# Five equal token blocks become four blocks of 512 local rows and one block of the 128 global rows

## The chip, the cores and the metric

One core of one Trainium2 chip runs the whole program. The metric is the device time of one execution in microseconds; the kernel before was run three times (890.51, 888.89 and 883.43 us, median 888.89).

## The reference

Attention with a band and global tokens feeds two feed-forward layers; 4 batches, 8 heads of 64, 512 local and 32 global positions each. Shortened:

```
k_all, v_all = [k_g, k_l], [v_g, v_l]                      # per batch and head
out_g = softmax(q_g @ k_all.T / 8) @ v_all                 # 32 global rows see all 544
s_ll  = where(|i - j| <= 32, q_l @ k_l.T / 8, -1e9)        # 512 local rows see a band
out_l = softmax([q_l @ k_g.T / 8, s_ll]) @ v_all           # ... and the 32 global keys
x = [out_g, out_l] as 4 * 544 = 2176 tokens of 512 features
h = x @ w_in            (512 -> 2048);  g = h if h > 0 else exp(h) - 1;          x = g @ w_out (2048 -> 512)
h = x @ w2_in           (512 -> 2048);  g = h if h >= 1 else 0 if h <= -1 else (h + 1)^2 / 4;  return g @ w2_out
```

Everything is float32. The kernel splits each factor of a layer's product into a high part and a low part (type float32r on the matmul) and forms a product by three matmuls: low weights with high activations, high with low, high with high.

## The kernel before, in words

**Attention (up to about 144 us).** 24 units of work (for each batch four pairs of heads of local rows and two quadruples of heads of global rows) run as a software pipeline whose order is written out by hand (class `Pinned`, line 109: instructions are kept in program order). A unit ends with transposes that lay its rows out as 128 features by tokens, and with `x_high` (line 281, ScalarE) and `x_low` (line 288, VectorE), which split them into the tiles `xh[j]` and `xl[j]` of token block `j`. The five blocks of 436, 436, 436, 436 and 432 tokens cut through the batches, so a unit's 512 local rows fall into two blocks and are copied in two pieces each (`spans`, line 63). Between the units, weights of the first three column groups are prepared and five products of the first layer are already computed (`early_ups`, line 608).

**Layers (from about 144 us).** Here instructions may be reordered by the scheduler of the language. A layer has 16 groups `f` of 128 of its 2048 inner features. They are taken in chunks of 3, 4, 3, 4, 2 (layer one) and 4, 3, 4, 3, 2 (layer two); within a chunk the loop runs over the token blocks `j` and inside over the `f` of the chunk (lines 700 to 718). One step (`f`, `j`) is:
- *up* (line 205): 12 matmuls, 4 slices of the contraction by 3 products, with 128 weight columns stationary and the tokens of the block moving, into one of four PSUM banks;
- `curve` and `join` (lines 211 to 228): the activation, two passes of ScalarE and one (layer one) or two (layer two) of VectorE;
- `high`, `low` (lines 230, 234): the split into `gh` (ScalarE) and `gl` (VectorE);
- *down* (line 270), three steps later (`LAG`): 12 matmuls, 4 output slices `d` by 3 products, into four banks `dn0` to `dn3`, which gather all `f` of the chunk;
- after the chunk's last `f`, `collect` (line 245): each bank is added to `acc[j]` on VectorE (the first chunk copies it on ScalarE). After the last chunk of layer one the sum is split again into `xh[j]`, `xl[j]` (lines 256, 257), after that of layer two it is written out, one transfer per block and slice (line 259).

**Weights.** Raw weights of one `f` are a transfer of 1 MB on the SP queue into a single raw buffer; two ScalarE and seven VectorE instructions then make the high and low tiles (`prep`, line 136). During a chunk, those of the next chunk are prepared, spread over its steps by `W_SHARE` (line 712). They go into a ring of seven tiles.

The code of the functions that the diff touches:

Of the kernel before, what the change touches and what calls it, by code (L numbers as in the profile page):

```python
# [58 lines left out]
W_SHARE = 0.8  # L59
WARM_UP = 10  # L60


def spans(t0, n):

    for j, (s, m) in enumerate(zip(STARTS, BLOCKS)):
        a, b = max(t0, s), min(t0 + n, s + m)
        if a < b:
            yield j, a - s, a - t0, b - a
# [3 lines left out]
def band_attention_then_two_mlps(  # L72
# [32 lines left out]
    xh = [xpool.tile([P, KT, n], F32R, name=f"xh{j}") for j, n in enumerate(BLOCKS)]  # L105
    xl = [xpool.tile([P, KT, n], F32R, name=f"xl{j}") for j, n in enumerate(BLOCKS)]
# [21 lines left out]
    slots = {}  # L128
# [3 lines left out]
    def add_slots(pool, numbers):  # L132
        for i in numbers:
            slots[i] = pool

    def prep(wraw_p, wtmp_p, layer, f, c0, n, raw_tag="wraw"):
# [5 lines left out]
        slot = (layer * NF + f) % WRING  # L142
        if (layer, f) not in wtiles:
            wtiles[layer, f] = [
                slots[slot].tile([P, WCOLS], F32R, tag=f"w{nm}{slot}", name="w" + nm) for nm in "hl"
            ]
# [41 lines left out]

    class Up:


        def __init__(self, layer, f, j):
            self.layer, self.f, self.j, self.n = layer, f, j, BLOCKS[j]
            self.k = 0
            early = count[0] < UP_EARLY or count[0] % 4 == 0
            count[0] += 1
            pool = ps_up[0 if early else 1]
            self.ps = pool.tile([P, BMAX], F32, tag="up", name="up")[:, :self.n]

        def products(self, m):  # L200
            wh, wl = wtiles[self.layer, self.f]
            for k in range(self.k, self.k + m):
                kt = k // 3
                w, x = ((wl, xh), (wh, xl), (wh, xh))[k % 3]
                eng.tensor.matmul(  # L205
                    self.ps, w[:, kt * P:(kt + 1) * P], x[self.j][:, kt, :],
                    start=k == 0, stop=k == 3 * KT - 1,
                )
            self.k += m

        def curve(self):
            self.g = t_p.tile([P, BMAX], F32, tag="g", name="g")[:, :self.n]
            if self.layer == 0:
                eng.scalar.activation(self.g, self.ps, AF.Exp)  # L214

                eng.scalar.activation(self.g, self.g, AF.Relu, bias=one_sb, scale=-1.0)  # L216
            else:
                self.e = t_p.tile([P, BMAX], F32, tag="e", name="e", bufs=1)[:, :self.n]
                eng.scalar.activation(self.g, self.ps, AF.Relu, bias=half_sb, scale=0.5)  # L219
                eng.scalar.activation(self.e, self.ps, AF.Relu, bias=nhalf_sb, scale=0.5)  # L220
# [8 lines left out]

        def high(self):  # L230
            self.gh = h_p.tile([P, BMAX], F32R, tag="gh", name="gh")[:, :self.n]
            eng.scalar.activation(self.gh, self.g, AF.Copy)  # L232

        def low(self):
            self.gl = h_p.tile([P, BMAX], F32R, tag="gl", name="gl")[:, :self.n]
            eng.vector.tensor_tensor(self.gl, self.g, self.gh.bitcast(F32), ALU.subtract)  # L236
            made[self.layer, self.f, self.j] = self.gh, self.gl
# [7 lines left out]
    def collect(layer, fs, j, d, ps):  # L245

        n = BLOCKS[j]
        first, last = fs[0] == 0, fs[-1] == NF - 1
        a = acc[j][:, d, :]
        if first:  # L250
            eng.scalar.activation(a, ps, AF.Copy)
        else:
            eng.vector.tensor_tensor(a, ps, a, ALU.add)  # L253
        if last and layer == 0:
            h = xh[j][:, d, :]
            eng.scalar.activation(h, a, AF.Copy)
            eng.vector.tensor_tensor(xl[j][:, d, :], a, h.bitcast(F32), ALU.subtract)
        elif last:
            eng.sync.dma_start(outT[d, :, STARTS[j]:STARTS[j] + n], a)

    def down(layer, fs, j, f, gs, banks, ds):

        n = BLOCKS[j]
        gh, gl = gs
        wh, wl = (w[:, KT * P:] for w in wtiles[layer, f])
        for d in ds:
            if f == fs[0]:
                banks[d] = ps_dn[d // 2].tile([P, BMAX], F32, tag=f"dn{d}", name="dn")[:, :n]
# [10 lines left out]


    def x_high(kts, t0, src):

        for j, o, so, n in spans(t0, src.shape[-1]):
            eng.scalar.activation(
                xh[j][:, kts[0]:kts[-1] + 1, o:o + n], src[:, :, so:so + n], AF.Copy
            )

    def x_low(kts, t0, src):

        for j, o, so, n in spans(t0, src.shape[-1]):  # L290
            at = (slice(None), slice(kts[0], kts[-1] + 1), slice(o, o + n))
            eng.vector.tensor_tensor(
                xl[j][at], src[:, :, so:so + n], xh[j][at].bitcast(F32), ALU.subtract
            )

    chunks = []
    for layer in range(2):
        f = 0
        for n in CHUNKS[layer]:
            chunks.append((layer, list(range(f, f + n))))  # L300
            f += n
# [4 lines left out]
    add_slots(ctx.enter_context(tc.tile_pool(name="w", bufs=1)), range(W_EARLY))  # L306
    acc[0] = xpool.tile([P, KT, BLOCKS[0]], F32, name="acc0")
# [3 lines left out]
    with ExitStack() as actx:  # L311
# [80 lines left out]
        def global_rows(b, g):  # L392
# [86 lines left out]
        def local_rows(b, hp):  # L479
# [219 lines left out]
    waiting = []  # L699
# [85 lines left out]
```

## Time and profile before

| | |
|---|---|
| median of three runs | 888.89 us |
| the profiled execution: span from first to last instruction | 889.8 us |
| TensorE matmul busy | 869.0 us (98%), 6458 matmuls |
| VectorE busy | 592.4 us (67%) |
| ScalarE busy | 445.1 us (50%) |
| GpSimd busy | 47.6 us (5%) |
| DMA | 65.51 MB, 74 GB/s on the mean |

The span is that of one profiled execution, which took 0.9 us more than the median of the runs; the page shows no further time around it. Busy time of TensorE counts each matmul from its start to a modelled end, and neighbours overlap, so a share of 98% says that something was always under way and not that the array was at its peak: for that the distance from one start to the next is read.

### The profile page before, as it was taken

How to read it: one execution, taken by the hardware profiler on the slowest of the kernel's cores; microseconds unless marked ns; L12 is line 12 of the kernel's file. 1: busy time of each engine (PE TensorE's matmuls, PEld its weight loads, DVE VectorE, ACT ScalarE, POOL GpSimd, SP SyncE). 2: the span in 40 equal slices, each digit the busy share in tenths (PEclk: the TensorE clock that was granted, in tenths of full speed). 3: DMA queues.
4: the chain of work that ended last, by engine and by line, in shares of the span. 5: the costliest groups of instructions: out<-in, count | busy, mean ns of one | idle time of the engine just before them, and what ended most of it. 6: DMA issues, size and time to landing. Idle time of an engine off the chain costs nothing.

```text
span 889.8 us, 15819 instructions
## 1 busy us (share of the span) xinstructions
PE 869.0 (98%) x6458; PEld 802.8 (90%) x6458; DVE 592.4 (67%) x1228; ACT 445.1 (50%) x845; POOL 47.6 (5%) x98
## 2 busy tenths in 40 slices
PE   8889889999999999999999999999999999999998
PEld 5667779999999999999999999999999999999997
DVE  5778755878534883873379995359859745845465
ACT  5667755766334543543356565456435433533332
POOL 4243220000000000000000000000000000000000
PEclk9998989999999999999999999999999999999999
DMA  8776741332100220120012111002201200000023
GB/s 283 223 252 222 233 137 55 121 110 95 48 0 1 95 96 1 48 95 1 0 48 88 56 48 48 1 1 95 95 1 48 95 1 1 1 1 0 1 75 127
DMA packets 17497, 65.51 MB, mean 74 GB/s; under 512 B 1936, under 2 KB 4752, under 8 KB 13712
## 3 DMA queue, kind: packets, MB, share of 16 engines
q1 hardware_dynamic: 17136, 64.23, 21.0%
q8 instruction: 51, 0.84, 0.4%
q10 hardware_dynamic: 288, 0.26, 0.1%
q14 instruction: 22, 0.18, 0.1%
HBM read 60.03 MB, written 4.46 MB: 72 GB/s over the span
## 4 chain that ended last, share of the span: by engine, by line
PE 94%; DMA 1%; issue 1%; ACT 1%; DVE 1%; POOL 1%; SPq 0%; POOLq 0%
PE dn L270 42%; PE up L205 41%; PE s L117 2%; PE pt L117 2%; PE po L117 1%; DMA k_sb<-in_kT 1%; PE up L117 1%; PE pog L117 1%; PE sg L117 1%; PE tg L117 1%; POOL kw L117 1%; PE ot L117 1%; ACT sn L117 1%; PE idle L117 0%; PE dn L117 0%
## 5 line engine op out<-in xcount | busy, mean ns | idle before, releaser
L270 PE MATMUL dn<-gh,wh 128*128 128x436 f32 (+1 forms) x634 | 228.2, 360 | 0.0
L270 PE MATMUL dn<-gh,wl 128*128 128x436 f32 (+1 forms) x634 | 226.8, 360 | 0.0
L270 PE MATMUL dn<-gl,wh 128*128 128x436 f32 (+1 forms) x634 | 224.9, 360 | 0.0
L205 PE MATMUL up<-xh,wl 128*128 128x436 f32 (+1 forms) x620 | 223.1, 360 | 0.0
L205 PE MATMUL up<-xh,wh 128*128 128x436 f32 (+1 forms) x620 | 223.0, 360 | 0.0
L205 PE MATMUL up<-xl,wh 128*128 128x436 f32 (+1 forms) x620 | 222.9, 359 | 0.0
L232 ACT ACTIVATE gh<-g 128x436 fp32r<-128x436 f32 (+1 forms) x155 | 88.0, 568 | 119.3 <-DVE g L228 72.4
L253 DVE TENSOR_TENSOR acc<-dn,acc 128x436 f32<-128x436 f32 (+1 forms) x160 | 93.2, 604 | 51.6 <-PE dn L270 51.4
L270 PEld LDWEIGHTS dn<-gl,wh 128*128 128x128 f32 x634 | 119.0, 188 | 6.6
L270 PEld LDWEIGHTS dn<-gh,wl 128*128 128x128 f32 x634 | 119.1, 188 | 6.5
L270 PEld LDWEIGHTS dn<-gh,wh 128*128 128x128 f32 x634 | 119.0, 188 | 6.3
L236 DVE TENSOR_TENSOR gl<-g,gh 128x436 fp32r<-128x436 f32 (+1 forms) x155 | 94.2, 608 | 45.1 <-ACT gh L232 43.1
L205 PEld LDWEIGHTS up<-xh,wl 128*128 128x128 f32 x620 | 116.4, 188 | 6.2
L205 PEld LDWEIGHTS up<-xl,wh 128*128 128x128 f32 x620 | 116.4, 188 | 6.2
L205 PEld LDWEIGHTS up<-xh,wh 128*128 128x128 f32 x620 | 116.4, 188 | 6.3
L219 ACT ACTIVATE g<-up,half_sb 128x436 f32<-128x436 f32 (+1 forms) x80 | 50.0, 624 | 123.0 <-PE up L205 116.2
L214 ACT ACTIVATE g<-up 128x436 f32<-128x436 f32 (+1 forms) x75 | 39.8, 532 | 107.0 <-PE up L205 107.0
L227 DVE SCALAR_TENSOR_TENSOR g<-g 128x436 f32<-128x436 f32 (+1 forms) x80 | 48.6, 607 | 64.1 <-ACT g L219 63.7
L225 DVE SCALAR_TENSOR_TENSOR g<-up,g 128x436 f32<-128x436 f32 (+1 forms) x75 | 45.4, 606 | 62.3 <-ACT g L216 62.2
L228 DVE TENSOR_TENSOR g<-g,e 128x436 f32<-128x436 f32 (+1 forms) x80 | 48.5, 606 | 3.7
L216 ACT ACTIVATE g<-g,one_sb 128x436 f32<-128x436 f32 (+1 forms) x75 | 49.3, 659 | 2.0
L220 ACT ACTIVATE e<-up,nhalf_sb 128x436 f32<-128x436 f32 (+1 forms) x80 | 49.3, 616 | 0.0
(89 smaller groups left out, 799.0 us busy)
## 6 DMA issues: line engine op xcount, KB each, us to landing
wraw<-in_w SPq DMA_DIRECT2D x29, 1024.0 KB, 4.8
v_sb<-in_vwin SPq DMA_DIRECT2D x32, 520.0 KB, 4.7
k_sb<-in_kT SPq DMA_DIRECT2D x16, 288.0 KB, 5.4
q_sb<-in_qT SPq DMA_DIRECT2D x16, 272.0 KB, 4.2
outT<-acc SPq DMA_DIRECT2D x16, 218.0 KB, 2.0
wraw<-in_w SPq DMA_DIRECT2D x6, 512.0 KB, 6.1
outT<-acc SPq DMA_DIRECT2D x4, 216.0 KB, 1.9
mask_sb<-in_mask ACTq DMA_DIRECT2D x1, 192.0 KB, 3.6
```

The lines of the kernel that those rows point to most:

```text
L117: return lambda *args, **kw: tc.keep_in_program_order(fn(*args, **kw))
L205: eng.tensor.matmul(self.ps, w[:, kt * P:(kt + 1) * P], x[self.j][:, kt, :], start=k == 0, stop=k == 3 * KT - 1,)
L216: eng.scalar.activation(self.g, self.g, AF.Relu, bias=one_sb, scale=-1.0)
L219: eng.scalar.activation(self.g, self.ps, AF.Relu, bias=half_sb, scale=0.5)
L220: eng.scalar.activation(self.e, self.ps, AF.Relu, bias=nhalf_sb, scale=0.5)
L225: eng.vector.scalar_tensor_tensor(g, self.ps, 0.0, g, ALU.max, ALU.subtract)
L227: eng.vector.scalar_tensor_tensor(g, g, 1.0, g, ALU.min, ALU.mult)
L228: eng.vector.tensor_tensor(g, g, self.e, ALU.add)
L232: eng.scalar.activation(self.gh, self.g, AF.Copy)
L236: eng.vector.tensor_tensor(self.gl, self.g, self.gh.bitcast(F32), ALU.subtract)
L253: eng.vector.tensor_tensor(a, ps, a, ALU.add)
L270: eng.tensor.matmul(banks[d], w[:, d * P:(d + 1) * P], g, start=f == fs[0] and k == 0, stop=f == fs[-1] and k == 2,)
```

## The change

Token blocks are now cut by kind: blocks 0 to 3 are the 512 local rows of each batch, and block 4 (`GR`) is the 4 times 32 global rows. `x_high` and `x_low` copy a unit's local rows in one piece. For the local blocks the steps are as before, with 512 moving columns in place of 436.

For the global block the operands change sides. *Up* is one product for a whole chunk: the 128 tokens (`xh[GR]` or `xl[GR]`) are stationary and the weights of all `m` groups of the chunk move, `m` times 128 columns. The activations then stand as tokens by features, so after `curve` and `join` they are turned by `m` TensorE transposes into another of the four *up* banks (`turn`), split from there by `high` and `low`, and used as stationary operand of *down* (`down_rows`): `3m` matmuls with all 512 output columns moving, into bank `dn3`. Its sum `acc[GR]` has tokens on the partitions; at the end of a layer four transposes (`turn_rows`) turn it back, for the next layer's `xh[GR]`, `xl[GR]` or for the output, which takes four transfers with pieces of 128 bytes.

The global step stands after the four local blocks in the first chunk and between blocks 1 and 2 in the others (`ORDERS`); `turn` follows one step later, `down_rows` three steps later, `turn_rows` two steps after that. The weight tiles of a chunk lie side by side in one tile of a ring of two (`add_ring`, 3 and 4 groups), so that the global step can read them as one operand. Preparing the weights begins two steps later in a chunk, and `W_SHARE` is 0.7.

```diff
-BLOCKS = [436, 436, 436, 436, 432]
-STARTS = [sum(BLOCKS[:i]) for i in range(len(BLOCKS))]
-BMAX = max(BLOCKS)
-NB = len(BLOCKS)
+GR = B
+NB = B + 1
+ORDERS = ((0, 1, 2, 3, GR), (0, 1, GR, 2, 3))
...
-WRING = 7
...
-W_EARLY = 3
+W_EARLY = CHUNKS[0][0]
...
-W_SHARE = 0.8
+W_SHARE = 0.7
...
+    sizes = [SL] * B + [B * SG]
+    xh = [xpool.tile([P, KT, n], F32R, name=f"xh{j}") for j, n in enumerate(sizes)]
+    xl = [xpool.tile([P, KT, n], F32R, name=f"xl{j}") for j, n in enumerate(sizes)]
...
+    def add_ring(pool, i):
+        n = max(len(fs) for _, fs in chunks[i::2])
+        ring[i] = [pool.tile([P, n, WCOLS], F32R, name=f"w{nm}{i}") for nm in "hl"]
+    def place(layer, f):
+        ci = next(i for i, (nl, fs) in enumerate(chunks) if nl == layer and f in fs)
+        return ring[ci % 2], f - chunks[ci][1][0]
...
+    def up_bank():
+        early = count[0] < UP_EARLY or count[0] % 4 == 0
+        count[0] += 1
+        return ps_up[0 if early else 1].tile([P, SL], F32, tag="up", name="up")
     class Up:
         def __init__(self, layer, f, j):
-            self.layer, self.f, self.j, self.n = layer, f, j, BLOCKS[j]
+            self.layer, self.f, self.j = layer, f, j
             self.k = 0
-            early = count[0] < UP_EARLY or count[0] % 4 == 0
-            count[0] += 1
-            pool = ps_up[0 if early else 1]
-            self.ps = pool.tile([P, BMAX], F32, tag="up", name="up")[:, :self.n]
+            if j == GR:
+                self.tiles, _ = place(layer, f[0])
+                self.m = len(f)
+            else:
+                self.m = KT
+            self.n = self.m * P
+            self.ps = up_bank()[:, :self.n]
         def products(self, m):
-            wh, wl = wtiles[self.layer, self.f]
+            if self.j == GR:
+                wh, wl = self.tiles
+            else:
+                wh, wl = wtiles[self.layer, self.f]
             for k in range(self.k, self.k + m):
                 kt = k // 3
                 w, x = ((wl, xh), (wh, xl), (wh, xh))[k % 3]
-                eng.tensor.matmul(
-                    self.ps, w[:, kt * P:(kt + 1) * P], x[self.j][:, kt, :],
-                    start=k == 0, stop=k == 3 * KT - 1,
-                )
+                x = x[self.j][:, kt, :]
+                if self.j == GR:
+                    w = w[:, 0:self.m, kt * P:(kt + 1) * P]
+                    out = self.ps.rearrange("p (f c) -> p f c", c=P)
+                    eng.tensor.matmul(out, x, w, start=k == 0, stop=k == 3 * KT - 1)
+                else:
+                    w = w[:, kt * P:(kt + 1) * P]
+                    eng.tensor.matmul(self.ps, w, x, start=k == 0, stop=k == 3 * KT - 1)
             self.k += m
...
+        def turn(self):
+            tp = up_bank()[:, :self.n]
+            for c in range(self.m):
+                eng.tensor.transpose(tp[:, c * P:(c + 1) * P], self.g[:, c * P:(c + 1) * P], eye_sb)
+            self.g = tp
...
+    def add_up(fs, a, ps):
+        if fs[0] == 0:
             eng.scalar.activation(a, ps, AF.Copy)
         else:
             eng.vector.tensor_tensor(a, ps, a, ALU.add)
-        if last and layer == 0:
+    def collect(layer, fs, j, d, ps):
+        a = acc[j][:, d, :]
+        add_up(fs, a, ps)
+        if fs[-1] < NF - 1:
+            return
+        if layer == 0:
             h = xh[j][:, d, :]
             eng.scalar.activation(h, a, AF.Copy)
             eng.vector.tensor_tensor(xl[j][:, d, :], a, h.bitcast(F32), ALU.subtract)
-        elif last:
-            eng.sync.dma_start(outT[d, :, STARTS[j]:STARTS[j] + n], a)
+        else:
+            eng.sync.dma_start(outT[d, :, j * S + SG:(j + 1) * S], a)
...
+    def down_rows(layer, fs, u):
+        ps = ps_dn[1].tile([P, SL], F32, tag="dn3", name="dn")
+        for i, f in enumerate(fs):
+            at = slice(i * P, (i + 1) * P)
+            wh, wl = (w[:, KT * P:] for w in wtiles[layer, f])
+            for k, (w, g) in enumerate(((wl, u.gh), (wh, u.gh), (wh, u.gl))):
+                eng.tensor.matmul(
+                    ps, g[:, at], w, start=i + k == 0, stop=f == fs[-1] and k == 2
+                )
+        add_up(fs, acc[GR], ps)
+    def turn_rows(layer):
+        tp = up_bank()
+        for d in range(KT):
+            at = slice(d * P, (d + 1) * P)
+            eng.tensor.transpose(tp[:, at], acc[GR][:, at], eye_sb)
+        tp = tp.rearrange("p (d t) -> p d t", d=KT)
+        if layer == 0:
+            eng.scalar.activation(xh[GR], tp, AF.Copy)
+            eng.vector.tensor_tensor(xl[GR], tp, xh[GR].bitcast(F32), ALU.subtract)
+        else:
+            a = acc[GR].rearrange("p (d t) -> p d t", d=KT)
+            eng.scalar.activation(a, tp, AF.Copy)
+            for d in range(KT):
+                rows = outT[d].rearrange("p (b s) -> p b s", b=B)[:, :, 0:SG]
+                eng.sync.dma_start(rows, a[:, d, :].rearrange("p (b r) -> p b r", b=B))
...
+    def x_high(j, kts, at, src):
+        eng.scalar.activation(xh[j][:, kts[0]:kts[-1] + 1, at], src, AF.Copy)
+    def x_low(j, kts, at, src):
+        at = (slice(None), slice(kts[0], kts[-1] + 1), at)
+        eng.vector.tensor_tensor(xl[j][at], src, xh[j][at].bitcast(F32), ALU.subtract)
...
+    acc[GR] = pool.tile([P, KT * P], F32, name="acc_rows")
...
+    def later(n, *what):
+        due.append((step + n, what))
+    def catch_up(now):
+        for item in [x for x in due if x[0] <= now]:
+            due.remove(item)
+            fn, *args = item[1]
+            fn(*args)
+    def turn_unit(layer, fs, u):
+        for part in (u.turn, u.high, u.low):
+            part()
+        later(LAG - 1, rows_unit, layer, fs, u)
+    def rows_unit(layer, fs, u):
+        down_rows(layer, fs, u)
+        if fs[-1] == NF - 1:
+            later(2, turn_rows, layer)
     for ci, (layer, fs) in enumerate(chunks):
-        tiles = [(nl, f) for nl, nfs in chunks[ci + 1:ci + 2] for f in nfs if (nl, f) not in wtiles]
-        steps, begun = NB * len(fs), 0
-        for j in range(NB):
-            banks = {} if ci + j else first
-            for i, f in enumerate(fs):
+        tiles = [(nl, f) for nl, nfs in chunks[ci + 1:ci + 2] for f in nfs]
+        order = [(j, f) for j in ORDERS[ci > 0] for f in (fs if j != GR else [fs])]
+        begun = 0
+        for i, (j, f) in enumerate(order):
+            if j == GR:
+                u = Up(layer, f, j)
+                u.products(3 * KT)
+                u.curve()
+                u.join()
+                later(1, turn_unit, layer, fs, u)
+            else:
+                if f == fs[0]:
+                    banks = {} if ci + j else first
                 if (layer, f, j) not in made:
                     up(layer, f, j)
                 ds = range(KT) if ci + j else range(KT // 2, KT)
-                waiting.append((layer, fs, j, f, made.pop((layer, f, j)), banks, ds))
-                if len(waiting) > LAG:
-                    down(*waiting.pop(0))
-                if begun < len(tiles) and (j * len(fs) + i) * len(tiles) >= begun * steps * W_SHARE:
-                    preps.append(prep(wraw_p, wtmp_p, *tiles[begun], 0, WCOLS))
-                    next(preps[-1])
-                    begun += 1
-                else:
-                    step_preps()
+                later(LAG, down, layer, fs, j, f, made.pop((layer, f, j)), banks, ds)
+            catch_up(step)
+            step += 1
+            at = i - LAG + 1
+            if begun < len(tiles) and at >= 0 and at * len(tiles) >= begun * len(order) * W_SHARE:
+                preps.append(prep(wraw_p, wtmp_p, *tiles[begun], 0, WCOLS))
+                next(preps[-1])
+                begun += 1
+            else:
+                step_preps()
         step_preps()
-    while waiting:
-        down(*waiting.pop(0))
+    while due:
+        catch_up(step)
+        step += 1
```

## Rows read from the trace of the kernel before

**Rows 1.** The page: the span; busy time of the engines.
```profile
span 889.8 us, 15819 instructions
...
PE 869.0 (98%) x6458; PEld 802.8 (90%) x6458; DVE 592.4 (67%) x1228; ACT 445.1 (50%) x845; POOL 47.6 (5%) x98
```

**Rows 2.** The page: the chain that ended last, by engine and by line.
```profile
PE 94%; DMA 1%; issue 1%; ACT 1%; DVE 1%; POOL 1%; SPq 0%; POOLq 0%
PE dn L270 42%; PE up L205 41%; PE s L117 2%; PE pt L117 2%; PE po L117 1%; DMA k_sb<-in_kT 1%; PE up L117 1%; PE pog L117 1%; PE sg L117 1%; PE tg L117 1%; POOL kw L117 1%; PE ot L117 1%; ACT sn L117 1%; PE idle L117 0%; PE dn L117 0%
```

**Rows 3.** Windows: stretch, its length, each engine's busy time (instructions), clock, DMA.
```profile
100.00:120.00 20.00, 17.16 (x356) 13.11 (x352) 14.41 (x61) 14.96 (x44) 6.61 (x14) 0.90 0.63 190
...
144.00:886.00 742.00, 742.00 (x3753) 703.93 (x3751) 492.71 (x774) 350.63 (x584) 0.00 (x0) 1.00 0.13 47
...
450.00:500.00 50.00, 50.00 (x255) 47.51 (x254) 46.28 (x73) 31.86 (x54) 0.00 (x0) 1.00 0.18 64
```

**Rows 4.** Groups by form, TensorE, 144 to 886 us: one of three alike each.
```profile
L270 PE MATMUL dn<-gh,wh 128*128 128x436 f32 x506 | 182.3, 360 | 0.0
...
L205 PE MATMUL up<-xh,wh 128*128 128x436 f32 x488 | 175.7, 360 | 0.0
...
L270 PE MATMUL dn<-gh,wl 128*128 128x432 f32 x128 | 45.9, 359 | 0.0
L205 PE MATMUL up<-xh,wl 128*128 128x432 f32 x128 | 45.8, 358 | 0.0
```

**Rows 5.** Windows: a stretch with matmuls of 436 columns alone.
```profile
204.69:264.22 59.53, 59.53 (x301) 56.33 (x300) 34.47 (x54) 26.73 (x43) 0.00 (x0) 1.00 0.15 54
```

**Rows 6.** Timeline of TensorE at the end: start, length; 436, then 432 columns.
```profile
876.66 0.36 PE L270 MATMUL dn<-gh,wl 128*128 128x436 f32 x1
...
881.41 0.36 PE L270 MATMUL dn<-gh,wl 128*128 128x432 f32 x1
...
885.94 0.36 PE L270 MATMUL dn<-gl,wh 128*128 128x432 f32 x1
```

**Rows 7.** The page: weight loads, busy and mean ns of one.
```profile
L270 PEld LDWEIGHTS dn<-gl,wh 128*128 128x128 f32 x634 | 119.0, 188 | 6.6
```

**Rows 8.** Timeline of TensorE: four transposes between products of a layer.
```profile
143.45 0.36 PE L117 MATMUL dn<-gl,wh 128*128 128x436 f32 x1
143.64 0.60 PE L117 MATMUL ot<-eye_sb,o_sb 128*128 128x128 f32 x4
144.00 0.45 PE L270 MATMUL dn<-gh,wl 128*128 128x436 f32 x1
144.28 0.36 PE L270 MATMUL dn<-gh,wh 128*128 128x436 f32 x1
```

**Rows 9.** Groups by form: copies and sums of VectorE and ScalarE at several widths.
```profile
L253 DVE TENSOR_TENSOR acc<-dn,acc 128x436 f32<-128x436 f32 x128 | 74.6, 605 | 46.1 <-PE dn L270 45.9
...
L117 DVE TENSOR_TENSOR xl<-ot,xh 128x432 fp32r<-128x432 f32 x4 | 2.4, 597 | 0.0
...
L117 DVE TENSOR_TENSOR xl<-ot,xh 128x108 fp32r<-128x108 f32 x4 | 1.0, 259 | 0.0
L117 DVE TENSOR_TENSOR xl<-ot,xh 128x80 fp32r<-128x80 f32 x4 | 1.0, 241 | 5.7 <-ACT xh L117 5.7
```

**Rows 10.** Groups by form: two of the seven VectorE instructions of one weight group.
```profile
L175 DVE SCALAR_TENSOR_TENSOR wl<-rest,power 128x1024 fp32r<-128x1024 uint32 x29 | 35.4, 1221 | 3.7 <-PE dn L270 3.0
...
L164 DVE TENSOR_SCALAR top<-top 128x1024 f32<-128x1024 f32 x29 | 19.9, 686 | 0.8 <-ACT top L157 0.8
```

**Rows 11.** The page: transfers, KB each, median us from issue to landing.
```profile
wraw<-in_w SPq DMA_DIRECT2D x29, 1024.0 KB, 4.8
...
outT<-acc SPq DMA_DIRECT2D x16, 218.0 KB, 2.0
```

**Rows 12.** Timeline of VectorE: its last instruction.
```profile
886.33 0.61 DVE L253 TENSOR_TENSOR acc<-dn,acc 128x432 f32<-128x432 f32 x1 [0.58 <-PE dn L270]
```

More of the change, by code (lines that the diff above doesn't have):

```diff
@@ L125, in band_attention_then_two_mlps @@
     eng = pinned
-    slots = {}
+    ring = {}
     wtiles = {}
     preps = []
-    def add_slots(pool, numbers):
-        for i in numbers:
-            slots[i] = pool
-    def prep(wraw_p, wtmp_p, layer, f, c0, n, raw_tag="wraw"):
[L142 to L146, printed above, removed]
+    chunks = []
+    for layer in range(2):
+        f = 0
+        for n in CHUNKS[layer]:
+            chunks.append((layer, list(range(f, f + n))))
+            f += n
+    def add_ring(pool, i):
[4 more added lines that the diff above has]
+        return ring[ci % 2], f - chunks[ci][1][0]
+    def prep(wraw_p, wtmp_p, layer, f, c0, n, raw_tag="wraw"):
+        tiles, at = place(layer, f)
+        wtiles[layer, f] = [w[:, at] for w in tiles]
         hi, lo = (w[:, c0:c0 + n] for w in wtiles[layer, f])
@@ L228, in join @@
                 eng.vector.tensor_tensor(g, g, self.e, ALU.add)
+        def turn(self):
[3 more added lines that the diff above has]
+            self.g = tp
         def high(self):
[L231 removed]
+            self.gh = h_p.tile([P, SL], F32R, tag="gh", name="gh")[:, :self.n]
             eng.scalar.activation(self.gh, self.g, AF.Copy)
         def low(self):
[L235 removed]
+            self.gl = h_p.tile([P, SL], F32R, tag="gl", name="gl")[:, :self.n]
             eng.vector.tensor_tensor(self.gl, self.g, self.gh.bitcast(F32), ALU.subtract)
[L237 removed]
+            if self.j != GR:
+                made[self.layer, self.f, self.j] = self.gh, self.gl
     def up(layer, f, j):
@@ L243, in up @@
             part()
[L245 to L250, printed above, removed]
+    def add_up(fs, a, ps):
+        if fs[0] == 0:
             eng.scalar.activation(a, ps, AF.Copy)
@@ L267, in down @@
             if f == fs[0]:
-                banks[d] = ps_dn[d // 2].tile([P, BMAX], F32, tag=f"dn{d}", name="dn")[:, :n]
+                banks[d] = ps_dn[d // 2].tile([P, SL], F32, tag=f"dn{d}", name="dn")
             for k, (w, g) in enumerate(((wl, gh), (wh, gh), (wh, gl))):
@@ L278, in down @@
                 collect(layer, fs, j, d, banks[d])
[L281 to L301, printed above, removed]
+    def down_rows(layer, fs, u):
[8 more added lines that the diff above has]
+        add_up(fs, acc[GR], ps)
@@ L608, in early_ups @@
         def early_ups():
-            for f, j in [(f, j) for j in range(NB) for f in chunks[0][1]][:UP_EARLY]:
+            for f, j in [(f, j) for j in range(B) for f in chunks[0][1]][:UP_EARLY]:
                 u = Up(0, f, j)
@@ L690, in band_attention_then_two_mlps @@
     pool = mpool("acc", 1)
-    for j in range(1, NB):
-        acc[j] = pool.tile([P, KT, BLOCKS[j]], F32, name=f"acc{j}")
+    for j in range(1, B):
+        acc[j] = pool.tile([P, KT, SL], F32, name=f"acc{j}")
+    acc[GR] = pool.tile([P, KT * P], F32, name="acc_rows")
     wraw_p = mpool("wraw", 1, side="right")
     wtmp_p = mpool("wtmp", 1, side="right")
-    add_slots(mpool("w_more", 1, side="right"), range(W_EARLY, WRING))
+    add_ring(mpool("w_more", 1, side="right"), 1)
     ps_up.append(mpool("ps_up", 3, space=PSUM))
     ps_dn.append(mpool("ps_dn1", 1, space=PSUM))
-    waiting = []
-    for ci, (layer, fs) in enumerate(chunks):
-        tiles = [(nl, f) for nl, nfs in chunks[ci + 1:ci + 2] for f in nfs if (nl, f) not in wtiles]
-        steps, begun = NB * len(fs), 0
-        for j in range(NB):
-            banks = {} if ci + j else first
-            for i, f in enumerate(fs):
+    due = []
+    step = 0
+    def later(n, *what):
[13 more added lines that the diff above has]
+            later(2, turn_rows, layer)
+    for ci, (layer, fs) in enumerate(chunks):
+        tiles = [(nl, f) for nl, nfs in chunks[ci + 1:ci + 2] for f in nfs]
[11 more added lines that the diff above has]
+                    banks = {} if ci + j else first
                 if (layer, f, j) not in made:
```

24 lines of the change are left out of this document (8 added, 16 removed).

## The prediction

> **What bounds the kernel now.** I began with the page: TensorE is busy 98% of the span, VectorE 67%, ScalarE 50% [rows 1], and the chain that ended last is 94% TensorE, of which the products of the two layers (lines 270 and 205) are 83% of the span [rows 2]. The windows then split the span. In the attention stage TensorE has gaps (17.16 of 20 us in the window shown); from 144 to 886 us it has none, 742.00 of 742.00 us, at a granted clock of 1.00 [rows 3]. So in the layers nothing is waited for, and the time is the number of matmuls times the distance between their starts. What a matmul costs there is therefore the question.
>
> **The price of one matmul.** By their forms 2982 matmuls of 436 columns (3 x 506 + 3 x 488) and 768 of 432 (6 x 128) run in that stretch [rows 4]. A stretch with 436 columns alone holds 300 starts (one of the 301 began before it) in 59.53 us: 198.4 ns each [rows 5]. The rest is for the 768: from 144.00 to the last start at 885.94 us are 741.94 us [rows 6, 8]; less 2982 x 0.1984 = 591.6 leaves 150.3 us, 195.7 ns each. The end of the trace has the same sign: 24 starts of 436 columns in 4.75 us (197.9 ns), then 23 of 432 in 4.53 us (197.0 ns) [rows 6]. Four columns less cost 0.9 to 2.7 ns less. One column per cycle of the 2.4 GHz clock would make 1.67 ns, in the middle, and I take that: a price of N/2.4 + 16.7 ns. With it, 16.7 ns hang on the matmul itself and not on its columns. The weight load beside each matmul takes 188 ns [rows 7], more than the 181.7 ns in which 436 columns stream, so it could be suspected as the bound; but then 432 columns would cost what 436 cost.
>
> **The change, part by part.**
>
> *Columns.* Before: 3072 matmuls of 436 and 768 of 432, 1,671,168 columns. After: 4 blocks x 32 groups x 24 = 3072 of 512; of the global block per layer 12 *up* matmuls for each of 5 chunks (two of 512, two of 384, one of 256 columns) and 48 *down* matmuls of 512. Together 3072 + 2 x (24 + 48) = 3216 of 512, 48 of 384 and 24 of 256: again 1,671,168 columns, in 3288 matmuls. Nothing is saved but the fixed price of 552 matmuls.
>
> *Local products and the wide global ones.* Before: 3072 x 198.4 + 768 x 195.7 = 759.8 us (90 of them lie before 144 us; they are priced alike on both sides). After: 3216 x (213.3 + 16.7 = 230.0) = 739.7 us. No row has 512 columns in this type, so the price has two ends: 215.6 ns if only the 2.3 ns that transposes show (below) stay on top of the stream, and 233.0 ns if the price grows in proportion (198.4 x 512 / 436). I take 230.0, by the nearest rows, those of 436 and 432.
>
> *Narrow global products.* 48 x (160 + 16.7) + 24 x (106.7 + 16.7) = 8.5 + 3.0 = 11.5 us. At least that, since the load is no shorter for them; at most 198.4 ns each, where a load of 188 ns is known to fit: 14.3 us, 2.8 more.
>
> *Transposes.* 16 per layer after the activations and 4 at its end: 40. The trace has four between two products: from the start of the one before, 143.45, to that of the second one behind, 144.28, are 830 ns; less two periods of 198.4 leaves 433 ns, 108 ns each, 4.3 us in all, with no further cost at either edge [rows 8]. As alone a stream of 128 columns and a load of 128 make 2 x 53.3 = 106.7 ns at 2.4 GHz, some 2 ns are left over. The Trainium skill (TensorE: Matmul & The Clock Gate, Part 4: PE-mode transpose) gives about 275 ns for a transpose in a kernel, by which the 40 would take an estimated 11 us and the change would gain nothing; the row has four in 0.60 us end to end, so what that figure counts overlaps.
>
> Sum on TensorE: 739.7 + 11.5 + 4.3 = 755.5, less 759.8: **-4.3 us**.
>
> *Waits that the global step adds.* Its transposes wait for `curve` and `join`, three instructions of about 0.6 us each (a sum of like width: 605 ns [rows 9]); cover is the next step's *up* and an older *down*, 24 periods or 5.5 us, and without cover TensorE's queue behind them would stand some 2 us in each of 10 chunks. `down_rows` takes bank `dn3` between two local blocks: the local sum ahead of it (0.6 us on VectorE [rows 9]) has one *up*, 2.8 us, as cover. The step takes two of the four *up* banks in place of one; they are free again three steps later. All costed at nothing.
>
> *VectorE and ScalarE.* Two widths of `xl` copies, 597 ns at 432 and 259 at 108 columns [rows 9], give 1.04 ns per column and 680 ns at 512. The layers' local instructions become four of 680 in place of five of 605: 10% less. Neither engine bounds the layers; worth nothing. In the attention each of 16 local units loses one `xh` and one `xl` piece (432 + 80 columns: 597 + 241 ns before against 680 [rows 9]), 16 x 0.16 = 2.5 us on VectorE and as much on ScalarE; as TensorE leads the chain there too, I count -0.5 us (ends 0 and -2.5).
>
> *Weights and transfers.* The same 29 transfers of 1 MB go through SP's queue and the one raw buffer, begun two steps later in a chunk; nothing since VectorE has slack, except at one place (rival 2). Output stays at 20 transfers, 16 + 4; the four global ones, 512 pieces of 128 bytes, are issued at least one step (24 x 230 ns = 5.5 us) ahead of the last matmul, where one of 218 KB lands in 2.0 us [rows 11]. Cost 0; at worst they hold up the last ones by 2 us. The tail, from the last matmul at 885.94 over the last sum (0.61 us from 886.33 [rows 12]) to 889.8, grows by that sum's 0.1 us. With these, +0.3 us.
>
> **Sum.** -4.3 - 0.5 + 0.3 = -4.5 us, 885.3 against the profiled 889.8. That execution lies 0.9 above the median of 888.89, so the forecast is **884.5 us**. Its own range: +2.8 and +2 from the bounds, -2.5 from the attention, and runs that spread from 883.43 to 890.51; 879 to 891.
>
> **Rivals.**
>
> 1. *The load goes out of the way (faster).* 188 ns of load [rows 7] outlast the stream at 436 columns, not at 512 (213.3 ns). If the 16.7 ns come of that, the price falls to 215.6: 3216 x 14.4 = 46.3 us more, 838 us. For it: load and period differ by only 10 ns. Against: 432 and 436 differ in period with the same load. The Trainium skill has a gap of N/2.4 + 2.5 ns (TensorE: Matmul & The Clock Gate, Back-to-back issue gap), by which 512 columns would take 215.8 ns; at 436 it says 184.2, and the trace's 198.4 disagrees. Chance 0.10.
>
> 2. *VectorE is late with the last weights of the first layer's last chunk (slower).* This chunk has 2 groups and prepares 4. By line 712's successor their transfers begin at steps 2, 4, 6 and 7 of 9 (before: 0, 2, 4, 6 of 10), so the third and fourth are both worked off in step 8. Each is 3 x 1.22 + 4 x 0.69 = 6.4 us of VectorE [rows 10], and the fourth transfer (4.8 us [rows 11]) waits for the raw buffer: about 16 us of queue. Behind it stand the sums that free the *down* banks; TensorE needs these within one step, 5.5 us, so it would stand 10.5 us: 895 us. It decides from a delay of 10 us on. For it: VectorE is busy 46.28 of 50 us near this place already [rows 3]. Against: TensorE lost nothing there, and VectorE's total falls. Chance 0.12.
>
> 3. *The price is in proportion to the columns.* Then 552 matmuls fewer save nothing: 3216 x 3.0 = 9.6 us more than forecast, 894 us; the transposes are the whole effect. For it: 2.7 ns for four columns is even above proportion (1.8). Against: 0.9 is below it. Chance 0.13.
>
> 4. *It does what it says and no more than noise shows*: the forecast. Chance 0.62; 0.03 is left for what I don't see.
>
> **How the numbers follow.** Differences of under 1% (8.9 us; 880.0 to 897.8) can't be told from none here. Faster: rival 1 and 0.15 of the forecast's chance, 0.20. Slower: 0.4 of rival 2, 0.2 of rival 3, and the remainder, 0.11. Within 1%: 0.69. The range, 876 to 898, takes in the forecast, rival 3 and most of rival 2, and leaves out rival 1.
>
> **What would show it.** Period between two starts of 512 columns: 230 ns (216: rival 1; 233 or more: rival 3). Four transposes in 0.43 us beyond the products around them. TensorE without a gap from 144 us on; a gap where layer one ends, with VectorE late, is rival 2. 3216 matmuls of 512 columns. The prediction is wrong if the period at 512 leaves 226 to 233 ns, or if TensorE stands still in the layers for more than 3 us.

## The result: 1.4% faster, the layers 17 us shorter

The changed kernel takes 875.62 us in the median of four runs, against 888.05 us for the kernel before beside it: a ratio of 0.9863, 95% interval 0.983 to 0.9896. Run again (e7 below) it took 873.51 against 889.94 us, 0.982 (0.9769 to 0.9871). The forecast was 884.5 us with a range from 876 to 898: the sign was right, the size was not, and the measured median lies 0.4 us below the range.

The page of the kernel after, its span and busy times, which answer to [rows 1], and the chain by line, to [rows 2]:

```profile
span 873.0 us, 14553 instructions
...
PE 852.3 (98%) x5946; PEld 699.1 (80%) x5946; DVE 583.4 (67%) x1130; ACT 432.2 (50%) x755; POOL 47.1 (5%) x98
...
PE dn L297 39%; PE up L224 38%; PE up L221 3%; PE dn L314 2%; PE s L107 2%; PE up L107 2%; PE pt L107 2%; PE po L107 2%; PE pog L107 2%; PE tg L107 1%; DMA v_sb<-in_vwin 1%; PE sg L107 1%; PE ot L107 1%; DMA wraw<-in_w 1%; PE idle L107 1%
```

The chain is the same, products of the layers on TensorE, with 512 matmuls fewer. Windows of the kernel after, columns as in [rows 3]: a stretch with 512 columns alone, the whole of the layers from the first to the last start, and the stretch where VectorE is fullest:

```profile
240.17:311.02 70.85, 70.85 (x315) 58.65 (x314) 45.68 (x63) 32.62 (x46) 0.00 (x0) 1.00 0.11 41
144.02:868.92 724.90, 724.90 (x3240) 601.69 (x3238) 484.01 (x691) 337.48 (x509) 0.00 (x0) 1.00 0.13 48
...
450.00:500.00 50.00, 50.00 (x230) 41.56 (x229) 47.71 (x72) 29.76 (x47) 0.00 (x0) 1.00 0.22 83
```

The layers begin at 144.0 us in both profiles and are 724.9 us long, where they were 741.9 [rows 6, 8]: all 17.0 us of the two profiled executions lie there (their spans differ by 16.8, the medians of the runs by 12.4). A run's time is some 1.8 us above its span (874.8 and 873.0 here), so the profiled execution of the kernel before took an estimated 891.6 us and lies 2.7 us above its median, not 0.9; the forecast, made as a difference, hardly moves by that. The profile shows no gap of TensorE in the layers. The groups by form from 144 to 869 us (one of three alike each) say how many matmuls these are:

```profile
L297 PE MATMUL dn<-gh,wh 128*128 128x512 f32 x506 | 196.9, 389 | 0.0
...
L224 PE MATMUL up<-xh,wl 128*128 128x512 f32 x488 | 190.8, 391 | 0.0
...
L314 PE MATMUL dn<-wl,gh 128*128 128x512 f32 x32 | 12.4, 389 | 0.0
...
L221 PE MATMUL up<-wl,xh 128*128 128x512 f32 x16 | 6.2, 389 | 0.0
...
L221 PE MATMUL up<-wh,xh 128*128 128x384 f32 x16 | 5.4, 337 | 0.0
...
L221 PE MATMUL up<-wh,xh 128*128 128x256 f32 x8 | 2.3, 282 | 0.0
```

3 x (506 + 488 + 32 + 16) = 3126 of 512 columns, 48 of 384, 24 of 256. The first window holds 312 of them (between two global steps) in 70.85 us, 227.1 ns each. From the total: 724.9 less 15.8 for the narrow ones and the transposes, as priced in the prediction, leaves 709.1 us, 226.8 ns each. The prediction had 230.0. That one number is worth 3126 x 3.2 = 10.0 us, and with 230.0 the layers would have been 734.8 us.

The transposes cost about what was said. Timeline of TensorE in the kernel after, start and length (one group of three):

```profile
190.94 0.39 PE L297 MATMUL dn<-gl,wh 128*128 128x512 f32 x1
191.17 0.49 PE L250 MATMUL up<-eye_sb,g 128*128 128x128 f32 x3
191.42 0.48 PE L224 MATMUL up<-xh,wl 128*128 128x512 f32 x1
191.73 0.39 PE L224 MATMUL up<-xl,wh 128*128 128x512 f32 x1
```

From 190.94 to 191.73 are 790 ns; less two periods of 226.8 leaves 336 ns, 112 each, as the 108 of [rows 8]. The tail, timelines of TensorE, VectorE and the SP queue at the end:

```profile
868.92 0.39 PE L297 MATMUL dn<-gl,wh 128*128 128x512 f32 x1
...
869.35 0.69 DVE L274 TENSOR_TENSOR acc<-dn,acc 128x512 f32<-128x512 f32 x1 [0.67 <-PE dn L297]
...
864.58 2.68 SPq L334 DMA_DIRECT2D outT<-acc_rows  x4
```

From the last matmul to the end are 4.1 us, 0.2 more than before, and the four transfers of global rows are issued before the last matmuls, as costed.

### The profile page after: what moved, and what is told of

It is laid out like the page before. It is cut to its first block, busy times and chain, and to the rows that moved or that the text cites. A ratio compares the mean times of both kernels' runs of the same rounds, so it can differ in the third digit from the quotient of the medians.

```text
span 873.0 us, 14553 instructions
## 1 busy us (share of the span) xinstructions
PE 852.3 (98%) x5946; PEld 699.1 (80%) x5946; DVE 583.4 (67%) x1130; ACT 432.2 (50%) x755; POOL 47.1 (5%) x98
## 4 chain that ended last, share of the span: by engine, by line
PE 95%; DMA 2%; issue 1%; DVE 1%; ACT 0%; SPq 0%
PE dn L297 39%; PE up L224 38%; PE up L221 3%; PE dn L314 2%; PE s L107 2%; PE up L107 2%; PE pt L107 2%; PE po L107 2%; PE pog L107 2%; PE tg L107 1%; DMA v_sb<-in_vwin 1%; PE sg L107 1%; PE ot L107 1%; DMA wraw<-in_w 1%; PE idle L107 1%
## 5 line engine op out<-in xcount | busy, mean ns | idle before, releaser
L297 PE MATMUL dn<-gh,wh 128*128 128x512 f32 x506 | 196.9, 389 | 0.0
L297 PE MATMUL dn<-gl,wh 128*128 128x512 f32 x506 | 196.8, 389 | 0.0
L297 PE MATMUL dn<-gh,wl 128*128 128x512 f32 x506 | 196.3, 390 | 0.0
L224 PE MATMUL up<-xh,wl 128*128 128x512 f32 x492 | 192.4, 391 | 0.0
L224 PE MATMUL up<-xl,wh 128*128 128x512 f32 x492 | 191.6, 390 | 0.0
L224 PE MATMUL up<-xh,wh 128*128 128x512 f32 x492 | 191.6, 389 | 0.0
L255 ACT ACTIVATE gh<-g 128x512 fp32r<-128x512 f32 x123 | 77.8, 632 | 118.6 <-DVE g L244 71.7
L274 DVE TENSOR_TENSOR acc<-dn,acc 128x512 f32<-128x512 f32 x128 | 84.9, 686 | 48.6 <-PE dn L297 48.4
L259 DVE TENSOR_TENSOR gl<-g,gh 128x512 fp32r<-128x512 f32 x123 | 84.7, 689 | 39.1 <-ACT gh L255 38.1
L235 ACT ACTIVATE g<-up,half_sb 128x512 f32<-128x512 f32 (+1 forms) x69 | 47.0, 681 | 113.9 <-PE up L224 104.9
```

What stands on the lines that cost most here:

```text
L224: eng.tensor.matmul(self.ps, w, x, start=k == 0, stop=k == 3 * KT - 1)
L297: eng.tensor.matmul(banks[d], w[:, d * P:(d + 1) * P], g, start=f == fs[0] and k == 0, stop=f == fs[-1] and k == 2,)
```

## The experiments

The question left by the result is why 512 columns cost 226.8 ns, 13.5 above their stream of 213.3, while 436 cost 198.3, 16.6 above theirs. Here the price of a matmul is the distance from its start to the next one's, its stream is N/2.4 ns for N moving columns (between 256 and 512 columns e5 has 106.7 ns for 256 columns, 0.417 each), and the surcharge is what the price has above the stream. The first four kernels are the kernel before with another line of block sizes or row distances.

**e1: blocks of 448 and 384.**

```diff
-BLOCKS = [436, 436, 436, 436, 432]
+BLOCKS = [448, 448, 448, 448, 384]
```

> The kernel before with blocks of 448, 448, 448, 448 and 384 tokens, nothing else changed: the same columns in the same 3840 matmuls, weights stationary. After the change a matmul of 512 columns started every 226.8 ns, 13.5 above its stream, where 436 had 16.6 above it. Theory A (rows): the 3 ns come of moving rows that don't begin at multiples of 64 bytes; 448 and 384 do, so 186.7 + 13.5 = 200.2 and 160 + 13.5 = 173.5 ns, the layers 11 us shorter than before (731 instead of 742 us). Theory B (count): the 3 ns come of a column count that isn't a multiple of 64; the same numbers. Theory C (load): they come where the stream is shorter than the weight load's 188 ns, as 186.7 and 160 are; then 203.3 and 176.6 ns, and the layers stay at 742 us.

Measured: 894.71 us, ratio 1.0082 (1.0036 to 1.0128). Windows, 300 matmuls of 448, 24 of 384, and the layers:

```profile
201.64:263.63 61.99, 61.99 (x301) 56.32 (x301) 35.98 (x55) 27.14 (x44) 0.00 (x0) 1.00 0.14 51
511.33:515.50 4.17, 4.17 (x25) 4.16 (x24) 2.23 (x4) 1.88 (x3) 0.00 (x0) 1.00 0.00 0
141.35:890.03 748.68, 748.68 (x3753) 693.39 (x3751) 491.75 (x774) 350.67 (x584) 0.00 (x0) 1.00 0.13 47
```

206.6 ns at 448, 20 above the stream, and 173.8 at 384, 13.8 above it: theories A and B had the second, none had the first. The same columns in the same number of matmuls are 6.7 us slower.

**e2: 436 columns in rows of 448 floats.**

```diff
-BMAX = max(BLOCKS)
+BMAX = 448
...
-    xh = [xpool.tile([P, KT, n], F32R, name=f"xh{j}") for j, n in enumerate(BLOCKS)]
+    xh = [xpool.tile([P, KT, BMAX], F32R, name=f"xh{j}")[:, :, :n] for j, n in enumerate(BLOCKS)]
```

(`xl` likewise.)

> The kernel before with the same 436 and 432 columns, but every row of the token tiles and of the activations 448 floats apart (1792 bytes, a multiple of 64) instead of 436. Theory A (rows): 195.2 ns at 436 and 193.5 ns at 432, the layers 12 us shorter. Theories B (count) and C (load): 198.3 and 196.2 ns as before, the layers 742 us.

Measured: 894.93 us in one run; the window with 300 matmuls of 436:

```profile
208.72:268.19 59.47, 59.47 (x302) 56.31 (x302) 34.54 (x54) 26.77 (x43) 0.00 (x0) 1.00 0.15 54
```

198.2 ns: at 436 columns this distance of the rows changes nothing, against theory A. The layers are 741.1 us by this trace; the run is longer in its attention stage, which ends at 148.2 us.

**e3: blocks of 500 and 176.** `BLOCKS = [500, 500, 500, 500, 176]`.

> The kernel before with blocks of 500, 500, 500, 500 and 176 tokens: rows of 2000 bytes, no multiple of 64 anywhere, but a stream of 208.3 ns, longer than the weight load. Theories A (rows) and B (count): 224.9 ns at 500 columns. Theory C (load): 221.8 ns. The 176 columns stream for 73.3 ns, less than the 108 ns that a load takes by the transposes: 87 to 90 ns if only the stream counts, 108 or more if the load does.

Measured: 909.16 us in one run. Windows, 300 matmuls of 500 and 24 of 176:

```profile
203.84:271.85 68.01, 68.01 (x303) 56.36 (x301) 37.75 (x55) 29.81 (x48) 0.00 (x0) 1.00 0.13 47
520.24:522.89 2.65, 2.65 (x26) 2.65 (x24) 1.49 (x3) 0.81 (x1) 0.00 (x0) 1.00 0.00 0
```

500 columns cost 226.7 ns, as much as 512, against theory C (221.8) and still 1.8 above theories A and B. 176 cost 110.4 ns, far above their stream of 73.3 and close to the 108 of a transpose: a floor. That the weight load makes it fits, but is not shown.

**e4: the new widths without the new operand order.** `BLOCKS = [512, 512, 512, 512, 128]`.

> The kernel before with blocks of 512, 512, 512, 512 and 128 tokens: the new widths without the new operand order, so no transposes of activations, and 768 matmuls of 128 columns with weights stationary. All theories: 226.8 ns at 512. At 128 the stream is 53.3 ns; if only that counts, 66.8 ns, 3072 x 226.8 + 768 x 66.8 = 748 us for all products against 760 before and 743 in the changed kernel, so some 5 us slower than the changed kernel. If the load of 108 ns is the bound, 768 x 108 = 83 and 780 us in all: 37 us slower than the changed kernel and 20 slower than before.

Measured: 915.29 us, ratio 1.0302 (1.0263 to 1.034). Windows, 300 matmuls of 512 and 24 of 128:

```profile
211.07:279.18 68.11, 68.11 (x302) 56.36 (x302) 37.14 (x53) 28.65 (x44) 0.00 (x0) 1.00 0.13 47
528.65:531.28 2.63, 2.63 (x26) 2.63 (x24) 2.63 (x4) 1.61 (x2) 0.00 (x0) 1.00 0.00 0
```

227.0 ns at 512, and 109.6 at 128, the floor again: 768 x 109.6 = 84 us for 128 rows, as the second case of the expectation had it. The layers are 764.7 us by this trace, 22.8 more than before. With this cut of the tokens the turned operands of the changed kernel are needed; they bring those 84 us down to some 49 (144 x 226.8 + 15.8 for the rest).

**e5: prices alone.** A kernel of its own: 48 matmuls of each width in a row, with a new load each, no other engine at work (shortened, the remarks added here; `WIDTHS` are 22 widths from 512 to 128).

```diff
+    for n in WIDTHS:
+        series(n, xa)                       # rows 512 floats apart
...
+    for n in (512, 500, 448, 436, 384):
+        series(n, xo[:, :, 2:2 + DM])       # rows 516 floats apart, 8 bytes off
+    for n in (512, 448, 436, 384):
+        series(n, xa, hold=3)               # three matmuls on the same weights
```

> Not the computation: only series of 48 matmuls of float32r with 128 stationary weight columns and from 512 down to 128 moving columns, into four banks, other engines idle; the output is zeros. At the end the same with moving rows 516 floats apart that begin 8 bytes off, and with three matmuls in a row on the same weights. Theory D (steps): the price has steps, because a matmul's stream and the load beside it meet again in a fixed pattern; where the count is a multiple of 128 it is the stream and 13.5 ns (226.9 ns at 512, 173.5 at 384, 118 at 256), between them up to 20 ns above it (206 at 448, 227 at 500, as at 512). Theory E (neighbours): the steps of the kernels come of what other engines and transfers do beside the matmuls; then the price here is the stream and one constant at every width, 13.5 ns or less, 200 ns at 448. The rows that begin off a multiple of 64 bytes change nothing by either. With weights held for three matmuls, 215.6 ns at 512 if the surcharge belongs to the change of weights; 226.9 if a load of the same weights costs the same.

Windows of one series of 48 each: widths 512, 480, 456, 436, 416, 400, 384, 256 and 192, then 512 with rows off, then 512 with weights held:

```profile
25.28:36.16 10.88, 10.88 (x49) 9.01 (x48) 0.00 (x0) 0.00 (x0) 0.00 (x0) 1.00 0.01 2
68.49:78.89 10.40, 10.40 (x50) 9.01 (x49) 0.00 (x0) 0.00 (x0) 0.00 (x0) 1.00 0.00 0
88.91:98.94 10.03, 10.03 (x49) 9.00 (x48) 0.00 (x0) 0.00 (x0) 0.00 (x0) 1.00 0.00 0
118.27:127.55 9.28, 9.28 (x49) 9.00 (x48) 0.00 (x0) 0.00 (x0) 0.00 (x0) 1.00 0.00 0
146.07:155.03 8.96, 8.96 (x49) 8.94 (x48) 0.00 (x0) 0.00 (x0) 0.00 (x0) 1.00 0.00 0
155.03:163.68 8.65, 8.65 (x50) 8.65 (x50) 0.00 (x0) 0.00 (x0) 0.00 (x0) 1.00 0.01 2
163.68:172.00 8.32, 8.32 (x50) 8.32 (x50) 0.00 (x0) 0.00 (x0) 0.00 (x0) 1.00 0.00 0
201.08:206.84 5.76, 5.76 (x51) 5.76 (x50) 0.00 (x0) 0.00 (x0) 0.00 (x0) 1.00 0.02 3
206.84:212.18 5.34, 5.34 (x51) 5.34 (x49) 0.00 (x0) 0.00 (x0) 0.00 (x0) 1.00 0.00 0
228.48:239.68 11.20, 11.20 (x50) 9.09 (x48) 0.00 (x0) 0.00 (x0) 0.00 (x0) 1.00 0.00 0
278.45:289.35 10.90, 10.90 (x49) 9.02 (x49) 0.00 (x0) 0.00 (x0) 0.00 (x0) 1.00 0.00 0
```

Per matmul from 512 to 256: 226.7, 216.7, 209.0, 193.3, 186.7, 180.2, 173.3 and 120.0 ns, above the stream by 13.3, 16.7, 19.0, 11.6, 13.3, 13.5, 13.3 and 13.3; 192 columns cost 111.3, hardly more than 128 in e4. 512 takes 227.1 ns (13.8 above) with weights held, and 233.3 (20 above) with rows off. So the surcharge is no constant even with nothing beside it, and theory E falls as it was put. Theory D holds at 512 and 384 and is 2 ns low at 256; at 448 and 500 it said 206 and 227, and the series gave 202.5 and 223.3. Nor are multiples of 128 the only cheap widths: 416 and 400 have the same surcharge. Against both, rows 8 bytes off cost 6 ns at 512 (and make 205.0 ns at 448, 200.2 at 436, both more than with rows in place). Holding the weights saves nothing at 512: each of these matmuls still has a load beside it (49 and 49 in the window).

**e6: the kernel before, widths that are multiples of 128.** `BLOCKS = [512, 512, 512, 384, 256]`.

> The kernel before with blocks of 512, 512, 512, 384 and 256 tokens, weights stationary throughout: widths that are multiples of 128 and no operand order changed, 3840 matmuls as before. By the prices measured so far 768 x (3 x 226.8 + 174.1 + 118.0) = 747 us for all products against 760 before and 745 in the changed kernel with its transposes: 13 us under before, within 3 us of the changed kernel. If the gain of the change belongs to the operand order and the 552 matmuls fewer, this kernel is no faster than before.

**e7: the changed kernel again, beside it.**

> The changed kernel, unedited, beside the one with 512, 384 and 256 tokens on the same chip: 875.6 us by its first runs, a ratio of 0.986 to the kernel before; layers of 724.9 us.

Measured: e6 877.91 us, ratio 0.9856 (0.9819 to 0.9893); e7 873.51 us, 0.982 (0.9769 to 0.9871). Windows of e6, 204 matmuls of 512 and its layers, then of e7, its layers:

```profile
199.91:246.18 46.27, 46.27 (x206) 38.30 (x205) 32.03 (x46) 22.05 (x35) 0.00 (x0) 1.00 0.20 69
...
141.69:871.96 730.27, 730.27 (x3752) 641.33 (x3751) 489.84 (x774) 349.82 (x584) 0.00 (x0) 1.00 0.13 48
```
```profile
143.50:868.41 724.91, 724.91 (x3241) 601.80 (x3239) 483.84 (x691) 337.11 (x509) 0.00 (x0) 1.00 0.13 48
```

One edited line takes the layers from 741.9 to 730.3 us, 11.7 of the 17.0 us, with all 3840 matmuls, with weights stationary and without a transpose. So two thirds of the gain in the layers are the price of the widths; the other 5.4 us are what the operand order and the fewer matmuls add (expected were 13 us less than before and at most 3 more than the changed kernel). No kernel here beats the changed one.

**e8: prices at the kernels' row distances.** As e5, with other tiles (the remark added here):

```diff
+CASES = (  # columns, distance between rows, first column
+    (512, 512, 0), (512, 512, 2), (512, 512, 4), (512, 512, 8), (512, 514, 0), (512, 516, 0), (512, 520, 0),
+    (512, 528, 0), (512, 544, 0), (512, 576, 0), (500, 500, 0), (500, 512, 0), (448, 448, 0), (448, 512, 0),
+    (436, 436, 0), (436, 448, 0), (436, 512, 0), (432, 432, 0), (432, 512, 0), (384, 384, 0), (384, 512, 0),
+)
```

> Not the computation: series of 48 matmuls of float32r alone, output zeros, as in the series of prices, now at several distances between rows and several first columns of the moving operand. Theory F (rows): the placing of the rows makes the difference between the series and the kernels, so at the kernels' distances (436, 432, 448 and 500 floats) the prices are those of the kernels, 198.3, 196.2, 206.3 and 227.3 ns, and lower at a distance of 512: 193 to 196 at 436 and 432, 202.5 at 448, 223.4 at 500. At 512 columns first columns of 2 and distances of 514 or 516 floats cost about 233 ns, distances of 528 and more (multiples of 64 bytes) 226.8. Theory G (work beside): the distance changes nothing at 436, 448 and 500 columns, and the kernels' prices come of the other engines and transfers.

Timeline of TensorE, in the order of the cases: one line per series of 48, so the distance between two starts by 48 is the price; ahead of it the window of the series (512, 512, 0), during which ScalarE still fills tiles of later series. Tile x__75 is (512, 512, 2), x__87 (512, 528, 0), x__89 (512, 544, 0), x__91 (512, 576, 0), x__95 has rows 448 apart, x__97 436, and x__73 512:

```profile
24.86:35.74 10.88, 10.88 (x50) 9.01 (x48) 0.00 (x0) 10.88 (x7) 0.00 (x0) 1.00 0.01 2
...
35.74 11.36 PE L51 MATMUL b<-x__75,wh 128*128 128x512 f32 x48
46.94 11.29 PE L51 MATMUL b<-x__77,wh 128*128 128x512 f32 x48
...
102.50 11.29 PE L51 MATMUL b<-x__87,wh 128*128 128x512 f32 x48
113.62 11.20 PE L51 MATMUL b<-x__89,wh 128*128 128x512 f32 x48
124.66 11.08 PE L51 MATMUL b<-x__91,wh 128*128 128x512 f32 x48
135.58 11.00 PE L51 MATMUL b<-x__93,wh 128*128 128x500 f32 x48
146.42 11.04 PE L51 MATMUL b<-x__73,wh 128*128 128x500 f32 x48
157.29 9.89 PE L51 MATMUL b<-x__95,wh 128*128 128x448 f32 x48
167.02 9.89 PE L51 MATMUL b<-x__73,wh 128*128 128x448 f32 x48
176.75 9.63 PE L51 MATMUL b<-x__97,wh 128*128 128x436 f32 x48
186.22 9.65 PE L51 MATMUL b<-x__95,wh 128*128 128x436 f32 x48
195.72 9.65 PE L51 MATMUL b<-x__73,wh 128*128 128x436 f32 x48
205.21 9.61 PE L51 MATMUL b<-x__99,wh 128*128 128x432 f32 x48
```

At 512 columns: 226.7 ns with rows 512 floats apart, 233.3 with the same rows 8 bytes off, 231.7 with rows 528 floats apart and 230.0 with 544 (multiples of 64 bytes, so theory F erred there), 227.5 with 576 (a multiple of 256 bytes). At 448 the distance changes nothing (202.7 both), nor at 436 (197.3 at 436, 197.7 at 512); 500 columns cost 225.8 at 500 and 226.5 at 512. So the placing of the rows counts at 512 columns, but it is not what parts the series from the kernels, as theory F had it. Theory G was right on the distances; that the rest comes of the other engines and transfers is not shown. 436 alone costs within 1 ns of what it costs in the kernel, though the same series (rows 512 apart) gave 193.3 ns in e5 and 197.7 here, so that some nanoseconds of scatter remain at this width (e5 itself has 197.7 with weights held), as at 500 (223.3 in e5, 226.5 here). 448 costs 4 ns less than in e1, which stays open.

**e9: the changed kernel with its rows off.**

```diff
-    xh = [xpool.tile([P, KT, n], F32R, name=f"xh{j}") for j, n in enumerate(sizes)]
+    xh = [xpool.tile([P, KT, n + 4], F32R, name=f"xh{j}")[:, :, 2:2 + n] for j, n in enumerate(sizes)]
...
-            self.gh = h_p.tile([P, SL], F32R, tag="gh", name="gh")[:, :self.n]
+            self.gh = h_p.tile([P, SL + 4], F32R, tag="gh", name="gh")[:, 2:2 + self.n]
```

(`xl` and `gl` likewise.)

> The changed kernel with the rows of its token tiles and of its activations 516 floats apart and beginning 8 bytes off, nothing else changed. Theory F (rows): the local matmuls of 512 columns rise from 226.9 to 230 to 233 ns, some 10 to 19 us in 2982 of them, most or all of what the change won; 886 to 892 us. If the column count alone makes the price, 226.9 ns and 875 us as in the changed kernel.

Measured: 894.96 us, ratio 1.0073 (1.0045 to 1.0101). Windows, 312 matmuls between two global steps (240.17 to 311.02 in the kernel after), 12 of the global *down* and the layers; below them the same 12 in the kernel after:

```profile
240.79:313.79 73.00, 73.00 (x316) 58.96 (x315) 45.79 (x64) 32.70 (x46) 0.00 (x0) 1.00 0.12 41
419.80:422.59 2.79, 2.79 (x13) 2.25 (x12) 1.32 (x2) 1.92 (x3) 0.00 (x0) 1.00 0.00 0
141.94:887.62 745.68, 745.68 (x3240) 604.95 (x3239) 484.83 (x691) 338.25 (x509) 0.00 (x0) 1.00 0.13 46
```
```profile
414.21:416.93 2.72, 2.72 (x14) 2.25 (x12) 1.39 (x2) 1.93 (x3) 0.00 (x0) 1.00 0.00 0
```

234.0 ns in place of 227.1, and layers of 745.7 us in place of 724.9, 20.8 more, above the 10 to 19 expected: two floats ahead of each row and two behind turn a gain of 1.4 to 1.8% into a loss of 0.7%. That the moving rows alone do this is not shown here: the global *down* rises too, from 226.7 to 232.5 ns, and what moves there are the weights, whose tiles the edit leaves as they are. Either the rows of the stationary operand count as well, or the longer tiles have shifted the weights in memory; e8 varies the moving rows alone.

## Why the prediction was wrong, step by step

- *What bounds the kernel.* Right: the layers are matmuls times their distance, before and after, with no gap of TensorE.
- *Columns and counts.* Right: 3288 matmuls, 3126 wide ones in the layers.
- *The price of one matmul.* **Here it failed.** The prediction made a line of two neighbouring widths, 436 and 432, took the 16.7 ns above the stream as fixed and carried it to 512: "I take 230.0, by the nearest rows, those of 436 and 432." Two rows four columns apart could not carry a line over 76 more: by its own reading of 0.9 to 2.7 ns for four columns, 512 lay anywhere between 215 and 250 ns. And the surcharge is not fixed. Alone it is 13.3 to 13.8 ns at 256, 384, 400, 416 and 512 columns, about 16 at 448, 17 at 480 and 19 at 456, and up to 20 at 512 when the rows are badly placed; in kernels it was 20 at 448 and 18.4 at 500. In the kernel the old widths cost 16.6 above their stream and the new one, with rows of exactly 2048 bytes, 13.5. In spans the forecast was 885.3 us and 873.0 came, 12.3 less. 3.2 ns by 3126 matmuls are 10.0 of these, nearly the whole distance between the forecast layers (734.8) and the measured ones (724.9). The bounds of the step, 215.6 and 233.0, did hold the value; the range did not make use of them, since the case between the ends was given no chance. Nor did its sign of being wrong fit its range: a period of 226 ns was still within the sign, and 4 ns by 3216 matmuls are 12.9 us, which makes 871.6 us, below the range.
- *The lower bound of that price, 215.6.* No run shows the 2.3 ns above the stream on which it rests; the lowest surcharge of the series shown is 11.6 ns. That a stream of 128 columns and a load make 53.3 ns each fits the 109.6 ns at 128 columns, but by it 176 columns would cost 73.3 + 53.3 = 126.7, and they cost 110.4.
- *Narrow products and transposes.* Right in size: by e1 and e5 384 and 256 columns cost 173.8 and 120.0 ns (priced at 176.7 and 123.4), a transpose 112 with its edges (108).
- *Added waits, VectorE, weights.* Costed at nothing, rightly: VectorE is busy 47.71 of 50 us where layer one ends, more than before [rows 3], and TensorE loses nothing there. Rival 2 did not come.
- *Attention.* A smaller miss. Besides the -0.5 us, the 90 early matmuls, "priced alike on both sides", put 90 x (230.0 - 198.4) = 2.8 us into this stage, where TensorE has gaps; it ends at 144.0 us in both profiles, so 2.3 us of the 12.3 lie here, and 0.1 in the tail. That the two ends agree so well is in part luck: in other profiles the stage ends between 141.4 us (e1) and 149.7 (e4), for the changed kernel itself at 143.5 (e7).
- *Rival 1* (the load goes out of the way): not so; 227 is not 215.6, weights held change nothing, and the 188 ns that the profile gives a load do not bound a matmul, since 256 columns start every 120.0 ns in e5. *Rival 3* (in proportion, 233.0): not so as a rule, though e9 lands near its number, by luck.

What stays open: why the surcharge depends on width and placement as it does, and why 448 columns cost 206.6 ns in e1 and 202.7 alone. Where the tiles begin in memory was not known, and no run varied it by itself.

## What to carry to other kernels

Where TensorE is the bound, the price of a matmul of another width is to be measured before it is planned with: a series of 48 in a bare kernel takes 10 us and would have given 227 here; at 448 it would have been 4 ns too low. A recut of blocks can win or lose more than the edit it belongs to (e1 +6.7 us, e6 -11.7 us in the layers, with the same work), so a change that also alters widths is compared with the old code at good widths. Of the distances tried for moving rows of 512 floats only 2048 and 2304 bytes, with nothing ahead of the first column, kept the price at 227 ns, and padding rows by a few floats can cost all that a change won (e9).

## What the runs showed of the hardware

- A float32r matmul with its load costs its stream at 2.4 GHz and 13.3 to 13.5 ns more at 256, 384, 400, 416 and 512 columns (120.0, 173.3, 180.2, 186.7, 226.7 ns), but 16.7 more at 480 (216.7) and 19.0 at 456 (209.0).
- The placing of the moving rows matters at 512 columns (226.7 to 233.3 ns in e8, and 233.3 with rows 8 bytes off in e5 too). Their distance made no difference at 448 (202.7 ns) and 436 (197.3 to 198.2 ns in e2 and e8).
- At narrow widths the price has a floor: 109.6 ns at 128 columns, 110.4 at 176, 111.3 at 192. That it is the weight load is likely and not shown.
- Three matmuls in a row on the same weights cost as much as with three different ones (227.1 and 226.7 ns at 512).
